# First two tiles of a spectral mixer normalized, turned and copied in three parts, x loaded tile by tile, last output in other pieces, and a new order of all work

## The chip, the cores and the metric

The kernel runs on one core of a Trainium2 chip. The metric is the device time of one execution in microseconds (us), as the median of a few runs. A core has five engines that work side by side and wait for each other through semaphores: TensorE (PE in the profile) multiplies matrices and turns tiles, VectorE (DVE) and ScalarE (ACT) do elementwise work, GpSimd (POOL) does a little, and SyncE (SP) issues the transfers (DMAs).

## The reference, cut to what matters

```python
xn = _layernorm(x, axis=-1)                     # x: 1 x 2048 x 640, bfloat16
return x + _A_ref(xn, A_w_r, A_w_i) + _B_ref(xn, B_w1, B_b1, B_w2, B_b2)

def _A_ref(x, w_r, w_i):                        # a filter in the 2-D spectrum
    X = rfft2(x.astype(float32)) * (w_r + 1j * w_i)
    return irfft2(X, s=(S, D)).astype(bfloat16)

def _B_ref(x, w1, b1, w2, b2):                  # a two-layer network
    h = gelu(x @ w1 + b1)                       # w1: 640 x 1536
    return h @ w2 + b2                          # w2: 1536 x 640
```

## The kernel before, in words

The 2048 rows of x are held as 16 tiles of 128 rows by 640 columns. Every tile is normalized, and its result goes two ways. For the network it is turned (columns to partitions, in five blocks of 128), because the matmuls with w1 need it so. For the spectrum it is folded twice by sums and differences, multiplied with tables of sines and cosines along the rows, then along the columns, filtered, and taken back.

Each piece of work is an operation with a name. Those that matter here, where `c` is a tile and `j` a block of 128 of its 640 columns:

- `x0`, `x1`, `x2`, `x4`, ... load x; from `x2` on two tiles in one transfer, so that `x14` brings tiles 14 and 15. `w1_00` to `w1_14` load w1 in two halves of five blocks.
- `st{c}` and `ag{c}` (DVE) take mean and variance. For tiles 0 and 1 `sq{c}` (ACT) and `rs{c}` (DVE) make the reciprocal root, for the others `ve` (DVE) and `rs` (POOL).
- `nm{c}` (DVE, L554) normalizes. In tile 0 it stands in two parts, columns 0 to 383 (`nm0`) and 384 to 639 (`nm0.3`).
- `tp{c}.{j}` (PE, L568) turns blocks of tiles 0 to 3 into a PSUM bank, one transpose each block, and `tc{c}.{j}` (DVE or ACT, L421/L422) copies them out. Tiles 4 to 15 are turned by DMA (`td{c}`, L560, issued on SP).
- `h{b}...` (PE) are the matmuls of the first layer. Blocks `h0` and `h1` are tiles 0 and 1 alone, taken row by row of w1, so that `h0.q.j` needs only block `j` of the turned tile and of w1. `h2` is tiles 2 and 3, `h3` is 4 and 5, `h4` is 6 and 7, `h5` is 8 to 11. `ge...` (ACT) is their gelu.
- `f1`, `f2` (DVE, L581 and L585) fold a pair of tiles, `G{c}` (PE) is the first spectral matmul of a tile and needs the folds of its pair. `f23` belongs to the tiles 6 and 7, and so to `G6` and `G7`.
- `k...`, `l...` (PE) are the second layer, `fin...` (PE) adds the last spectral matmul into the same bank, `os...` (DVE, L811) adds x and writes the result, `out...` (SP, L818) stores it.
- `idle0` and `idle1` are matmuls on a tile of zeros whose result nobody reads: 38 before the first data, and four between the turning of tile 0 and that of tile 1.

Nothing decides an order while the kernel runs. A table of some 900 entries, `ORDER`, names engine and operation one after the other, and `SLOTS` names the PSUM bank or buffer of each. Each engine takes its own entries strictly in this order; an operation that waits holds up all that stand behind it on its engine. A transfer too waits in SP's list until its data is ready.

Of the kernel before, what the change touches and what calls it, by code (L numbers as in the profile page):

```python
# [254 lines left out]
sp:w1_11 dve:ag1 dve:nm0 act:sq1 pe:b1mm dve:nm0.3 sp:w1_12 pe:tp0.0 dve:rs1 pe:tp0.3 dve:nm1 pe:idle1 sp:w1_13 act:tc0.3 dve:tc0.0 pe:tp1.0 act:b1cp
sp:w1_14 dve:f10.1 pe:h0.0.0 pe:h0.0.1 act:tc1.0 sp:x4 dve:f10.0 pe:h0.1.0 pe:h0.1.1 sp:x6 pe:h0.0.2 act:table1 pe:h0.1.2 pe:h1.1.0 sp:g pe:h1.1.1
pe:h1.1.2 pe:h1.0.0 sp:x8 pe:h1.0.1 dve:st3.1 pe:h1.0.2 sp:x10 dve:st3.0 pe:h1.0.3 pe:h0.0.3 sp:x12 dve:st2.1 pe:h1.1.3 pe:h0.0.4 pe:h1.0.4 dve:ag3
dve:st2.0 pe:h1.1.4 act:ge0.0 pe:h0.2.0 act:ge1.0 pe:h1.3.0 dve:ve3 dve:f20.11 pe:h0.3.0 act:ge1.4 pool:rs3 dve:ag2 dve:f20.10 pe:h0.2.1 act:ge1.5
pe:h0.1.3 dve:ve2 pe:h0.1.4 act:ge1.3 dve:f20.00 pe:h1.2.0 pool:rs2 act:ge0.1 pe:h1.3.1 dve:nm3 pe:h0.3.1 act:ge0.5 pe:h1.2.1 dve:f20.01 act:ge0.4
pe:h0.3.2 dve:nm2 act:ge0.2 pe:h0.2.2 pe:h0.2.3 pe:h0.2.4 dve:f11.0 pe:tp2.0 act:ge0.6 dve:f11.1 pe:h0.3.3 pe:h1.3.2 act:tc2.0 pe:tp3.0 dve:st4.0  # L260
pe:h1.2.2 dve:st4.1 pe:h1.2.3 act:tc3.0 pe:h0.3.4 pe:h1.3.3 dve:st5.0 pe:h1.2.4 act:ge1.2 pe:h1.3.4 dve:st5.1 pe:h2.4.0 act:ge1.7 act:ge1.8 pe:h2.4.3
dve:ag4 dve:ag5 act:ge1.1 pe:h2.8.0 dve:ve4 act:ge0.11 dve:f21.11 pe:h2.8.3 pool:rs4 dve:f21.00 act:ge1.6 pe:h2.9.0 dve:f21.10 act:ge0.3 pe:h2.9.3
act:ge0.7 pool:xbpad0b pe:h2.6.0 dve:nm4 act:ge1.10 pe:h2.6.3 dve:nm5 act:ge1.9 sp:td4 pe:h2.7.0 act:ge0.8 dve:f21.01 pe:h2.7.3 dve:st6.1 act:ge1.11
pe:h2.5.0 act:ge0.10 dve:st11.0 act:ge2.9 pe:G1 dve:f12.1 pe:h2.5.3 act:ge2.8 sp:td5 pe:h2.10.0 dve:st7.1 act:ge2.6 pe:h2.10.3 dve:st8.1 act:ge2.7
pe:h2.2.0 pe:G0 act:ge2.5 dve:f12.0 pe:h2.2.3 sp:x14 dve:st10.0 act:gx0.0 pe:h2.0.0 sp:w2_0 pe:h2.11.0 dve:st7.0 pe:h2.11.3 sp:W00m dve:st11.1
pe:h2.3.0 act:ge2.4 dve:st10.1 pe:h2.3.3 pe:h2.0.3 dve:f22.00 act:ge2.3 pe:h2.1.0 dve:st6.0 pe:h2.1.3 act:ge2.2 pe:h3.6.0 dve:f22.01 act:ge2.0 dve:ag6
dve:ag7 pe:h3.4.0 dve:f22.11 act:ge2.1 dve:ve6 dve:ag11 pe:G3 dve:f22.10 pool:rs6 pe:h3.6.3 dve:ag10 pe:G2 pe:h3.4.3 dve:nm6 act:gx1.0 pe:h3.5.0
dve:st9.0 pe:h3.7.0 sp:td6 dve:ve10 pe:h3.7.3 dve:st12.0 pool:rs10 pe:h3.8.0 dve:st8.0 act:ge2.10 pe:h3.8.3 pe:h3.9.0 act:ge2.11 dve:nm7 pe:h3.9.3
dve:nm10 sp:td7 pe:G4 act:ge3.9 dve:st9.1 pe:h3.5.3 pe:h3.0.0 dve:ag8 act:ge3.5 dve:ag9 pe:h3.0.3 dve:f13.0 pe:G5 act:ge3.4 dve:ve8 sp:td10 dve:st14.1
pe:h3.1.0 act:ge3.8 pool:rs8 pe:h3.1.3 dve:f13.1 act:gx2.0 pe:k1.0.0 dve:nm8 pe:k1.0.3 dve:f23.11 sp:td8 dve:nm11 pe:h3.2.0 act:ge3.1 dve:f23.01  # L270
dve:nm9 pe:h3.2.3 act:ge3.0 pe:h3.3.0 dve:f23.10 act:ge3.6 pe:h3.3.3 dve:f23.00 pe:h3.10.0 sp:td9 act:ge3.2 pe:h3.10.3 dve:f14.1 pe:h3.11.0 act:ge3.7
dve:f14.0 pe:h3.11.3 act:ge3.3 pe:G7 dve:f24.10 act:ge3.10 sp:td11 pe:G6 dve:st14.0 act:ge3.11 pe:h4.4.0 dve:st15.0 act:gx3.0 pe:h4.6.0 sp:w2_1
pe:h4.6.3 dve:f24.01 dve:f24.00 pe:h4.7.0 sp:W01p dve:f24.11 pe:h4.10.0 dve:ag14 dve:st15.1 pe:h4.7.3 pe:h4.10.3 dve:ag15 act:ge4.6 pe:h4.11.0
sp:bias2 dve:st13.1 pe:h4.11.3 act:ge4.7 sp:e dve:f15.1 pe:G9 act:ge4.10 pe:h4.4.3 dve:f15.0 sp:W11n pe:h4.5.0 act:ge0.9 dve:st12.1 act:ge4.11
pe:h4.5.3 sp:W10n pe:G8 dve:ag12 pe:h5.3.0 dve:st13.0 act:gx4.0 sp:W03n dve:ve14 dve:f25.00 pool:rs14 pe:h5.3.3 dve:f25.10 sp:W11p pe:h5.1.0 dve:ag13
act:ge5.3 dve:nm15 sp:W10m dve:ve12 pe:h5.1.3 dve:f25.01 pool:rs12 dve:f25.11 sp:W13p pe:h5.5.0 act:ge5.1 dve:nm13 sp:W01n pe:h5.5.3 act:ge4.5
dve:nm12 pe:h5.2.0 act:ge4.4 sp:W02p dve:f16.1 act:ge5.5 pe:G10 dve:nm14 sp:W00n pe:h5.2.3 dve:f16.0 sp:td15 pe:G11 dve:f26.01 act:ge5.2 pe:h4.2.0
dve:f26.11 dve:f26.00 pe:h4.2.3 dve:f26.10 pe:k1.0.6 dve:f17.0 sp:td13 pe:h5.4.0 dve:f17.1 pe:k1.0.9 dve:xs0 pe:h4.3.0 sp:td14 pe:h5.4.3 dve:kk1.0
# [573 lines left out]
```

## Time and profile before

| | us |
|---|---|
| median of 3 runs | 148.09 (147.81 to 149.21) |
| the profiled execution | 147.38 |
| its span | 146.1 |
| PE busy | 142.4 (97%) |
| DVE busy | 116.6 (80%) |
| ACT busy | 79.7 (55%) |

The span is what the profiler saw between the first and the last instruction; 1.28 us of the profiled execution lie around it. PE is busy nearly all the time, but its matmuls overlap in time, so this share alone does not say how closely they follow each other. The chain of waits says that, and so does the distance of the starts of equal matmuls.

### The profile page before, as it was taken

Reading aid. Unit: us, or ns where it says so; the run is one execution under the profiler, and the core shown is the slowest. Engines: PE = TensorE matmul, PEld = TensorE weight load, DVE = VectorE, ACT = ScalarE, POOL = GpSimd, SP = SyncE. Lnnn points to the kernel's source line nnn. Section 1 sums busy time; section 2 is a strip of 40 time slices with the busy share of each in tenths; the row PEclk is TensorE's granted clock in tenths of the full one; section 3 lists DMA queues with packets and bytes.
Section 4 is the critical chain, followed back from the end, with each engine's and each line's share of the span. In section 5 each row is a group of like instructions: output and inputs, shape, how many; then the busy total and the mean of one; then the engine's idle time right before and its main releaser. Section 6 shows DMA issues by size and latency. Waiting matters only on the chain.

```text
span 146.1 us, 4167 instructions
## 1 busy us (share of the span) xinstructions
PE 142.4 (97%) x1760; PEld 99.9 (68%) x1760; DVE 116.6 (80%) x272; ACT 79.7 (55%) x149; POOL 7.3 (5%) x24
## 2 busy tenths in 40 slices
PE   7999999999999999999999999999999999999993
PEld 7899889896659776546464443456678677767782
DVE  2999898999899486679899978840279979496993
ACT  3389997998747651578674787881043734100000
POOL 2031103102100000000000000000000000000000
PEclk9999999999999999999999999999999999999999
DMA  4999588698999999000000568267500022021334
GB/s 129 312 384 404 141 194 257 124 74 228 282 234 174 173 178 259 11 4 0 4 2 4 114 120 129 50 131 79 109 0 0 4 85 97 4 77 57 135 134 140
DMA packets 29226, 18.40 MB, mean 126 GB/s; under 512 B 20248, under 2 KB 27928, under 8 KB 29080
## 3 DMA queue, kind: packets, MB, share of 16 engines
q1 hardware_dynamic: 29184, 18.14, 52.5%
q8 instruction: 14, 0.23, 0.7%
q14 instruction: 4, 0.03, 0.1%
q10 hardware_dynamic: 24, 0.00, 0.0%
HBM read 10.92 MB, written 2.62 MB: 93 GB/s over the span
## 4 chain that ended last, share of the span: by engine, by line
PE 95%; DVE 2%; DMA 2%; issue 0%
PE ps L411 93%; DMA X<-in_A_x_dram 2%; DVE U L522 1%; PE ps L568 1%; DVE W L811 0%; DVE T L554 0%; DVE mv L524 0%; DVE rstd L528 0%
## 5 line engine op out<-in xcount | busy, mean ns | idle before, releaser
L411 PE MATMUL ps<-W,gT 128*128 128x256 bf16 (+3 forms) x396 | 58.8, 296 | 0.0
L411 PE MATMUL ps<-xnT,W 128*128 128x256 bf16 (+2 forms) x420 | 57.8, 288 | 0.0
L411 PEld LDWEIGHTS ps<-W,gT 128*128 128x128 bf16 x396 | 36.8, 98 | 15.3 <-issue 1.2
L411 PEld LDWEIGHTS ps<-xnT,W 128*128 128x128 bf16 x420 | 34.4, 98 | 15.2 <-issue 2.4
L640 ACT ACTIVATE gT<-ps,b1col 128x256 bf16<-128x256 f32 (+2 forms) x84 | 36.7, 522 | 8.5 <-PE ps L411 8.4
L421 ACT ACTIVATE Wf<-ps 128x960 bf16<-128x960 f32 (+1 forms) x9 | 7.6, 880 | 17.2 <-PE ps L411 17.2
L522 DVE BATCH_NORM_STATS2 U<-X 128x6 f32<-128x320 bf16 x32 | 14.1, 475 | 2.6 <-DMA X<-in_A_x_dram 2.6
L421 ACT ACTIVATE T<-ps 128x644 bf16<-128x644 f32 (+2 forms) x17 | 9.3, 581 | 8.0 <-PE ps L411 8.0
L421 ACT ACTIVATE XV<-ps 128x1280 bf16<-128x1280 f32 (+1 forms) x8 | 9.5, 1193 | 1.3 <-PE ps L411 1.3
L585 DVE TENSOR_TENSOR T<-T 128x128 bf16<-128x128 bf16 (+1 forms) x32 | 9.0, 311 | 0.1
L811 DVE TENSOR_TENSOR W<-ps,xnT 128x256 bf16<-128x256 f32 (+1 forms) x16 | 7.4, 481 | 1.4 <-DMA out_dram<-W 1.2
L554 DVE TENSOR_SCALAR T<-X,mv,rstd 128x640 bf16<-128x640 bf16 (+2 forms) x17 | 7.0, 433 | 1.6 <-POOL rstd L533 1.3
L422 DVE CAST T<-ps 128x644 bf16<-128x644 f32 x7 | 5.8, 828 | 2.9 <-PE ps L411 2.8
L801 DVE TENSOR_TENSOR xnT<-ps,X 128x384 f32<-128x384 f32 (+1 forms) x16 | 7.7, 484 | 0.6 <-PE ps L411 0.3
L421 ACT ACTIVATE Xb<-ps 128x960 bf16<-128x960 f32 x5 | 6.2, 1262 | 3.4 <-PE ps L411 3.4
L411 PE MATMUL ps<-Wf,htab 128*128 128x256 bf16 (+3 forms) x33 | 8.0, 296 | 0.0
L533 POOL TENSOR_TENSOR rstd<-ve,mhalf 128x2 f32<-128x2 f32 (+1 forms) x8 | 6.1, 768 | 29.1 <-DVE ve L532 29.1
L700 DVE TENSOR_TENSOR T<-T 128x644 bf16<-128x644 bf16 x16 | 7.4, 485 | 0.1
L581 DVE TENSOR_TENSOR T<-T 128x640 bf16<-128x640 bf16 x16 | 7.3, 480 | 0.1
L411 PE MATMUL ps<-EB,XV 32*128 32x160 bf16 (+1 forms) x128 | 7.2, 232 | 0.0
L411 PEld LDWEIGHTS ps<-EB,XV 32*128 32x128 bf16 (+1 forms) x128 | 5.5, 95 | 2.2 <-ACT Xb L421 0.5
L774 DVE TENSOR_TENSOR Wf<-Wf 128x960 bf16<-128x960 bf16 (+1 forms) x12 | 6.8, 595 | 0.1
(62 smaller groups left out, 127.0 us busy)
## 6 DMA issues: line engine op xcount, KB each, us to landing
out_dram<-W SPq DMA_DIRECT2D x15, 160.0 KB, 1.8
X<-in_A_x_dram SPq DMA_DIRECT2D x7, 320.0 KB, 6.6
W<-in_B_w_dram SPq DMA_DIRECT2D x10, 192.0 KB, 4.3
W<-in_B_w_dram SPq DMA_DIRECT2D x2, 960.0 KB, 6.2
Wf<-in_A_w_r_dram SPq DMA_DIRECT2D x7, 160.5 KB, 5.9
Wf<-in_A_w_i_dram SPq DMA_DIRECT2D x7, 160.5 KB, 4.3
gtab<-c_G SPq DMA_DIRECT2D x1, 512.0 KB, 7.4
htab<-c_H SPq DMA_DIRECT2D x1, 512.0 KB, 5.4
```

The source lines that it names most:

```text
L411: ins = e.matmul(o_, lhsT=lw, rhs=rh, start=st, stop=sp_, skip_group_check=True)
L421: return e.activation(dst(), src(), ACT.Copy)
L522: K.op(f"st{c}.{h}", "dve", lambda e, _, c=c, h=h: e.bn_stats(stats[:, c, 6 * h:6 * h + 6], view(X, c * D + H2 * h, [[1, H2]])), reads=[B_ ...
L533: K.op(f"rs{c0}", "pool", lambda e, _, a=a, b=b: e.tensor_tensor(out=rstd[:, a:b], in0=ve[:, a:b], in1=mhalf[:, a:b], op=ALU.pow), reads=[ ...
L554: norm = K.op(f"nm{c}" if not a else f"nm{c}.3", "dve", lambda e, _, c=c, n=n, a=a, b=b, xnv=xnv: e.tensor_scalar(out=xnv(n, a, [[1, b - a ...
L581: K.op(f"f1{pair}.{k}", "dve", lambda e, _, k=k, op=op, xnv=xnv, x1v=x1v: e.tensor_tensor(out=x1v(H2 * k, [[D, 2], [1, H2]]), in0=xnv(0, 0 ...
L585: ring_ops.append(K.op(f"f2{pair}.{k}{i}", "dve", lambda e, _, op=op, x1v=x1v, xfv=xfv, o_=o_, o0=o0, o1=o1, w=w: e.tensor_tensor(out=xfv( ...
L640: K.op(f"ge{bi}.{fc}", "act", lambda e, _, c0=c0, nt=nt, fc=fc, f0=f0, hps=hps: e.activation(gT[:, fc, 128 * c0:128 * (c0 + nt)], psb(hps. ...
L700: return e.tensor_tensor(out=rows, in0=rows, in1=view(TT, TB.slot * 4 * KP + r * KP, [[2 * KP, 2], [1, KP]]), op=op)
L774: K.op(f"yf{gi}.{k}", "dve", lambda e, _, k=k, op=op, y2=y2, yf=yf, n=n: e.tensor_tensor(out=view(Wf, YF + yf.slot * 3 * D + (D - 1) * k, ...
L801: K.op(f"kk{c}.{o0}", "dve", lambda e, _, kps=kps, c=c, home=home, o0=o0, w=w: e.tensor_tensor(out=home[:, o0 // 128:(o0 + w) // 128], in0 ...
L811: K.op(f"os{c}.{o0}", "dve", lambda e, _, c=c, os_=os_, fps=fps, o0=o0, w=w, kept=kept, home=home if kept else None: e.tensor_tensor(out=( ...
```

## The change

Tiles 0 and 1 are now both treated in three parts, of one, two and two blocks of 128 columns: three normalizations, three turns (in three banks), three copies each. The matmuls of `h0` and `h1` wait for the part that holds their block. `idle1` is gone. Tiles 2 and 3 are loaded by two transfers, `x2` and `x3`, of which the second stands behind the first half of w1. The last output tile, 15, is finished in pieces of 384, 160 and 96 columns instead of 320, 160 and 160. One more group of output tiles gets a copy (`xr1`) of the block of 128 rows that its matmuls use in quarters. The whole table of the order is new, and 29 copies changed between DVE and ACT.

```diff
+PARTS = (0, 1, 3, 5)
-NEAR = (2, 3, 4, 5)
+NEAR = (1, 2, 3, 4, 5)
-PIECES = {15: [(0, H2), (H2, Q4), (H2 + Q4, Q4)]}
-WARM = (38, 4)
+PIECES = {15: [(0, 384), (384, 160), (544, 96)]}
+WARM = 38
 ORDER = """
-act:table0 pool:id1 sp:w1_00 sp:w1_01 sp:w1_02 sp:x2 dve:st0.0 dve:st0.1 sp:w1_03 dve:st1.1 sp:w1_04 dve:ag0 dve:st1.0 sp:w1_10 act:sq0 dve:rs0
...
-        for j in range(5):
-            if j == 3:
-                first(load_x(2, 2))
-            first(load_w1(0, j))
-        for j in range(5):
-            first(load_w1(1, j))
+        for h in range(2):
+            for j in range(5):
+                if (h, j) in ((0, 3), (1, 0)):
+                    first(load_x(2 + h, 1))
+                first(load_w1(h, j))
...
-        B_xnT = [[K.buf(f"xnT{c}.0"), K.buf(f"xnT{c}.3")] for c in range(16)]
+        B_xnT = [[K.buf(f"xnT{c}.{a}") for a in PARTS[:-1]] for c in range(16)]
...
-                parts = ((0, 384), (384, D)) if c == 0 else ((0, D),)
+                parts = [(128 * a, 128 * b) for a, b in zip(PARTS, PARTS[1:])] if c < 2 else [(0, D)]
...
-                for j0, j1, engs in ((0, 3, "dve"), (3, 5, "act")) if c == 0 else ((0, 5, "dve act"),):
+                for k, (j0, j1) in enumerate((a // 128, b // 128) for a, b in parts):
...
-                    if j0:
-                        idle("idle1", WARM[1], gate=[tp])
-                    K.op(f"tc{c}.{j0}", engs, copy(
+                    K.op(f"tc{c}.{j0}", "dve act", copy(
...
-                                reads=[B_w1s[h][j], B_xnT[c0][j // 3]], writes=[banks[q]], gate=l1_of[bi][-2:][:1] if j else []))
+                                reads=[B_w1s[h][j], B_xnT[c0][(j + 1) // 2]], writes=[banks[q]], gate=l1_of[bi][-2:][:1] if j else []))
```

Two places show what the new order does. The first is the start of PE's list, with what each instruction waits for (`EB` holds the zeros and the unit matrix, `T` the normalized tile, `xnT` the turned one, `W` is w1). Before:

```order
L411 MATMUL ps<-EB 128x128 x37
L411 MATMUL ps<-EB 128x12 [waits d_bias1,s_pool]
L568 MATMUL ps<-EB,T 128x128 [waits s_dve]
L568 MATMUL ps<-EB,T 128x128 x2
L568 MATMUL ps<-EB,T 128x128 [waits s_dve]
L568 MATMUL ps<-EB,T 128x128
L411 MATMUL ps<-EB 128x128 x4
L568 MATMUL ps<-EB,T 128x128 [waits s_dve]
L568 MATMUL ps<-EB,T 128x128 x4
L411 MATMUL ps<-xnT,W 128x128 [waits d_w1_00,s_dve]
```

The same place after:

```order
L413 MATMUL ps<-EB 128x12 [waits d_bias1,s_pool]
L569 MATMUL ps<-EB,T 128x128 [waits s_dve] x2
L569 MATMUL ps<-EB,T 128x128
L569 MATMUL ps<-EB,T 128x128 [waits s_dve]
L569 MATMUL ps<-EB,T 128x128
L413 MATMUL ps<-xnT,W 128x128 [waits d_w1_00,s_act,s_dve]
L413 MATMUL ps<-xnT,W 128x128 x2
L569 MATMUL ps<-EB,T 128x128 [waits s_dve]
L413 MATMUL ps<-xnT,W 128x128 x3
L569 MATMUL ps<-EB,T 128x128 [waits s_act,s_dve]
```

The four matmuls on zeros are gone, and the first six matmuls of the first layer stand before and between the turns of tile 1.

The second place is DVE's list between the statistics of tiles 8 to 13 and the normalization of tile 6 (`d_x10`, `d_x12`, `d_x14` are the landings of these loads of x; L522 and L523 are `st`, L581 and L580 `f1`, L585 and L584 `f2`, L554 and L555 `nm`). Before, from `nm6` to `st14.1`:

```order
L554 TENSOR_SCALAR T<-X,mv,rstd 128x640 [waits s_pool]
L522 BN_STATS U<-X 128x6
L532 TENSOR_SCALAR ve<-mv 128x2 [waits s_dve]
L522 BN_STATS U<-X 128x6 [waits d_x12]
L522 BN_STATS U<-X 128x6
L554 TENSOR_SCALAR T<-X,mv,rstd 128x640
L554 TENSOR_SCALAR T<-X,mv,rstd 128x640 [waits d_td4,d_td5,s_pool]
L522 BN_STATS U<-X 128x6
L524 BN_AGGR mv<-U 128x2 [waits s_dve] x2
L581 TENSOR_TENSOR T<-T 128x2x320
L532 TENSOR_SCALAR ve<-mv 128x2 [waits s_dve]
L522 BN_STATS U<-X 128x6 [waits d_x14]
```

After, from `f12.0` to `nm6`:

```order
L580 TENSOR_TENSOR T<-T 128x2x320 [waits s_dve]
L523 BN_STATS U<-X 128x6 x3
L523 BN_STATS U<-X 128x6 [waits d_x14]
L523 BN_STATS U<-X 128x6
L525 BN_AGGR mv<-U 128x2 [waits s_dve]
L580 TENSOR_TENSOR T<-T 128x2x320
L525 BN_AGGR mv<-U 128x2
L533 TENSOR_SCALAR ve<-mv 128x2 [waits s_dve]
L584 TENSOR_TENSOR T<-T 128x2x2x128 [waits s_pe]
L584 TENSOR_TENSOR T<-T 128x2x2x32
L584 TENSOR_TENSOR T<-T 128x2x2x128
L555 TENSOR_SCALAR T<-X,mv,rstd 128x640 [waits s_pool]
```

The first use of `x14` stood behind the normalizations of the tiles 6, 7 and 10 and the first sums of the pair of tiles 6 and 7; it is now `st15.0`, ahead of all of them, and everything behind it on DVE waits for that load. In SP's list `x14` stands right behind `td5` in both kernels.

More of the change, by code (lines that the diff above doesn't have):

```diff
@@ L255 @@
[L255 to L278, printed above, removed]
@@ L314 @@
+pe:fin15.544 sp:out14.0 dve:os15.544 sp:out15.544
 """
 SLOTS = """
-idle0:0 b1ps:1 xn0:0 x10:0 xf0:0 tps0.0:2 tps0.3:3 idle1:0 tps1.0:4 aps0:0 xn1:1 x11:0 xf1:1 tps2.0:7 tps3.0:5 aps1:0 xn2:2 x12:0 xf2:0 aps2:0 xn3:3
-x13:0 xf3:1 aps3:0 xn4:0 x14:0 xf4:0 aps4:0 xn5:2 x15:0 xf5:1 aps5:0 xn6:0 x16:0 xf6:0 aps6:0 xn7:1 x17:0 xf7:1 aps7:0 hps0_0:5 hps0_1:6 hps0_2:0
-hps0_3:3 hps1_0:4 hps1_1:7 hps1_2:2 hps1_3:1 hps2_0:4 hps2_2:5 hps2_4:7 hps2_6:4 hps2_8:5 hps2_10:6 hps3_0:6 hps3_2:4 hps3_4:5 hps3_6:7 hps3_8:4
@@ L327 @@
-kps10_384:6 fps10_0:1 fps10_384:4 yo4:0 y24:0 yf4:0 eps4:0 xr4:1 os11:3 kps11_0:7 kps11_384:7 fps11_0:6 fps11_384:1 os12:2 fps12_0:0 fps12_384:3
-os13:0 fps13_0:4 fps13_384:5 yo5:0 y25:0 yf5:0 eps5:0 xr5:0 os14:0 fps14_0:7 fps14_384:6 os15:2 fps15_0:0 fps15_320:1 fps15_480:4
+idle0:0 b1ps:1 xn0:0 x10:0 xf0:0 tps0.0:2 tps0.1:3 tps0.3:0 tps1.0:2 tps1.1:3 tps1.3:5 aps0:0 xn1:1 x11:0 xf1:1 tps2.0:7 tps3.0:4 aps1:0 xn2:2 x12:0
+xf2:0 aps2:0 xn3:3 x13:0 xf3:1 aps3:0 xn4:1 x14:0 xf4:0 aps4:0 xn5:0 x15:0 xf5:1 aps5:0 xn6:2 x16:0 xf6:0 aps6:0 xn7:3 x17:0 xf7:1 aps7:0 hps0_0:1
@@ L446, in idle @@
             pe(name, lambda: [(psb(b.slot, [[1, 128]]), warm, warm, True, True) for _ in range(n)], reads=[B_warm], writes=[b], **kw)
-        idle("idle0", WARM[0])
+        idle("idle0", WARM)
         B_b1, B_b2b = K.buf("b1t"), K.buf("b2")
```

124 lines of the change are left out of this document (76 added, 48 removed).

## The prediction

> **What bounds the kernel now.** I read the chain of waits first, in order of time, since it says what set the end.
>
> ```profile
> 0.73 2.31 DMA X<-in_A_x_dram
> 3.07 1.28 DVE U L522 x3
> ...
> 5.09 0.32 DVE T L554
> 5.46 0.72 PE ps L568 x5
> ...
> 6.94 5.36 PE ps L411 x96
> ...
> 13.20 46.73 PE ps L411 x485
> 59.93 83.62 PE ps L411 x1059
> 143.57 0.32 DVE W L811
> ```
>
> From 5.46 us on the chain never leaves PE until the last sum at 143.57 us. So a change can win in three places alone: ahead of the first useful matmul, in the count and width of PE's matmuls, and behind the last one. Everywhere else it can only lose, by making PE wait. The timeline of the first microseconds comes next; PE's rows of the same time are merged over equal forms.
>
> ```profile
> 5.46 0.72 PE L568 MATMUL ps<-EB,T 128*128 128x128 bf16 x5
> 5.76 0.45 DVE L554 TENSOR_SCALAR T<-X,mv,rstd 128x640 bf16<-128x640 bf16 x1
> 5.97 0.63 PE L411 MATMUL ps<-EB 128*128 128x128 bf16 x4
> 6.13 0.35 DVE L422 COPY xnT<-ps 128x384 bf16<-128x384 bf16 x1
> 6.39 0.55 PE L568 MATMUL ps<-EB,T 128*128 128x128 bf16 x5
> 6.78 5.52 PE L411 MATMUL ps<-xnT,W 128*128 128x128 bf16 x96
> ```
>
> Two things are to be seen. The four `idle1` matmuls stand between the turns of tiles 0 and 1, for 6.39 - 5.97 = 0.42 us. And PE changes its pace there: the starts of the four lie (0.63 - 0.31) / 3 = 0.107 us apart, taking 0.31 us for one of them from the row of `idle0` (`EB`) below, and those of the first layer (5.52 - 0.22) / 95 = 0.056, with 0.22 us for one. The change falls between 6.4 and 6.7 us. All of them have the same 128 x 128 form.
>
> ```profile
> L411 PE MATMUL ps<-EB 128*128 128x128 bf16 x23 | 2.9, 314 | 0.0
> L411 PE MATMUL ps<-xnT,W 128*128 128x128 bf16 x94 | 5.4, 219 | 0.0
> ```
>
> The end is read from the timeline too. SP issues five stores in a row there:
>
> ```profile
> 142.44 2.45 SPq L818 DMA_DIRECT2D out_dram<-W  x5
> 142.47 0.99 PE L411 MATMUL ps<-W,gT 128*128 128x160 bf16 x12
> 143.30 0.23 PE L411 MATMUL ps<-Wf,htab 128*128 128x160 bf16 x1
> out_dram<-W SPq DMA_DIRECT2D x2, 40.0 KB, 1.6
> ```
>
> Five issues in 2.45 us put the last one at about 144.4, half a microsecond behind the end of the last sum (143.57 + 0.32 = 143.89). It lands 1.6 us later, and the span ends at 146.1. From the start of the last matmul to the end of the span it takes 146.1 - 143.30 = 2.8 us.
>
> **The start.** Up to `nm0` DVE does the same as before. The normalizations by size:
>
> ```profile
> L554 DVE TENSOR_SCALAR T<-X,mv,rstd 128x640 bf16<-128x640 bf16 x1 | 0.4, 445 | 0.0
> L554 DVE TENSOR_SCALAR T<-X,mv,rstd 128x384 bf16<-128x384 bf16 x1 | 0.4, 378 | 0.0
> L554 DVE TENSOR_SCALAR T<-X,mv,rstd 128x256 bf16<-128x256 bf16 x1 | 0.3, 339 | 0.0
> 5.02 0.64 DVE L554 TENSOR_SCALAR T<-X,mv,rstd 128x384 bf16<-128x384 bf16 x2
> ```
>
> 256 columns more cost 67 ns (445 - 378), so a part of 128 takes about 0.31 us, and as the pair in the last row overlaps by 0.08 us, its successor starts after 0.23. A part of 256 hands on after 0.26. Walked from 5.02: the three parts of tile 0 end at 5.33, 5.59 and 5.85. In the rows `nm1` starts 0.1 us behind the end of the pair (5.76 against 5.66), with `rs1` between; here I put `tc0.0` there, at about 5.85, to end near 6.1 (0.35 us for three times the columns before), and tile 1's parts from 6.0 on, to end at 6.31, 6.57 and 6.83. PE follows a part after 0.05 us (5.46 against 5.41). One block is turned at 5.38, two at 5.65, two at 5.9; the first three matmuls of the layer run from 6.13 to 6.45, a turn to 6.56, three matmuls to about 6.75, and the last turns wait for 6.83 and end near 7.0. Six matmuls of the layer are then done, worth 6 x 0.056 = 0.34, which puts the layer's start at 6.66 in the old reckoning, against 6.78: **-0.12 us**. Of the 0.42 us of `idle1` the rest is not won, because tile 1's normalization, not PE, is then late. Bounds: -0.42, and +0.1 in an execution where PE's pace is already 0.056 at 5.4 (the last turns then wait for 6.83 just the same).
>
> DVE pays for it. Six parts cost 2 x (0.23 + 0.26 + 0.26) = 1.5 us of it where three cost 0.30 + 0.26 + 0.36 = 0.92, and a copy of tile 1 is added: it is about **0.65 us later** from here on. The loads of w1 have cover: `x2` is half as large ahead of the fourth block of w1, and `x3` only fills the place of the other half further on.
>
> **DVE and the load x14.** This is where that delay can reach PE. The new order puts `st15.0` ahead of the normalizations of tiles 6 to 11.
>
> ```profile
> 18.10 0.58 SPq L406 DMA_DIRECT2D X<-in_A_x_dram  x1
> X<-in_A_x_dram SPq DMA_DIRECT2D x1, 320.0 KB, 3.8
> 19.00:20.00 1.00, 1.00 (x12) 1.00 0.90 93
> 20.00:21.00 1.00, 1.00 (x11) 1.00 0.62 114
> 21.00:22.00 1.00, 1.00 (x13) 1.00 1.04 393
> q8 instruction: 1, 0.02, 2.9%
> ```
>
> `x14` lands at 18.10 + 3.8 = 21.9; the last column of the three windows (GB/s) shows that it hardly moves for two microseconds, behind `td5` and one packet of 0.02 MB on an instruction queue, and then goes at 393. The Trainium skill (Runtime: NRT & Kernel Launch, Instruction fetch mechanics) says that an engine's program is fetched in 16 KiB blocks at a cost that is mostly hidden. By that rule alone the load would not be late and this whole term zero; the trace has the slow windows at that packet, without showing which of the two made them.
>
> These rows give the pieces of DVE's work from there on, and the place of `G6` and `G7` on PE:
>
> ```profile
> 18.75 1.66 DVE L522 BATCH_NORM_STATS2 U<-X 128x6 f32<-128x320 bf16 x4
> 29.07 0.89 DVE L581 TENSOR_TENSOR T<-T 128x640 bf16<-128x640 bf16 x2
> 28.29 0.75 DVE L585 TENSOR_TENSOR T<-T 128x512 bf16<-128x512 bf16 x2
> 27.30 0.21 DVE L585 TENSOR_TENSOR T<-T 128x128 bf16<-128x128 bf16 x1
> 24.27 0.79 DVE L554 TENSOR_SCALAR T<-X,mv,rstd 128x640 bf16<-128x640 bf16 x2
> 13.38 0.33 DVE L524 BATCH_NORM_AGGREGATE mv<-U 128x2 f32<-128x12 f32 x2
> 21.50 0.17 DVE L532 TENSOR_SCALAR ve<-mv 128x2 f32<-128x2 f32 x1
> 22.65 0.45 DVE L554 TENSOR_SCALAR T<-X,mv,rstd 128x640 bf16<-128x640 bf16 x1 [0.47 <-POOL rstd L533]
> 29.80 0.72 PE L411 MATMUL ps<-gtab,T 128*128 128x128 bf16 x10
> ```
>
> Before, the first user of `x14` comes four microseconds after it landed. At 18.75 (first row) DVE had four `st` of the tiles from 6 on and two `f1` behind it; ahead of `st15.0` stand ten and one. That is 18.75 + 6 x 0.40 - 0.40 = 20.75, or 21.4 with the 0.65: DVE comes before the load and stands.
>
> Behind that start come, up to the end of the sum that `G6` needs (`f23.00`): five `st`, three `f1`, seven `f2`, four `nm`, six `ag`, three `ve`, and one more `f2`. From start to start they take 0.40, 0.40, 0.33 (0.13 for a small `f2`, 0.21 less the overlap), 0.36, 0.13 and 0.07 us: 2.0 + 1.2 + 1.0 + 0.5 + 1.4 + 0.8 + 0.2 + 0.42 = 7.5. `nm6` starts 1.15 us behind its `ve6` (22.65 against 21.50, through POOL); only 0.8 us of `f2` lie between them, so 0.35 is added: 7.9. PE comes to these two `G` (29.80, x10) about 0.12 earlier than before, at 29.7. They wait if `x14` lands after 29.7 - 7.9 = 21.8. It is issued behind `td5`, which comes up to 0.65 later, so at 18.1 to 18.75. Nearest row: 3.8 us, so 21.9 to 22.55, a wait of 0.1 to 0.75; if nothing stands in its way, the 2.3 us of the first load of x (160 KB) and 0.4 for its second half at 393 GB/s make 20.8 to 21.45, and the wait is nothing. I take 22.2, so 0.4, and 0.1 for `G4` and `G9`, which follow on the same engine: **+0.5 us**, bounds 0 and +1.0. The first `h5`, which needs the last of `td8` to `td11`, is pushed by the same wait and so covered.
>
> **Width of the last tile.** The columns are the same, but 12 matmuls of 96 columns may not run at 96/160 of the 0.069 us that the rows of 160 give ((0.99 - 0.23) / 11); between 0.041 and the 0.056 of 128 columns the loss is 0 to 12 x 0.015 = 0.18. I take **+0.08**. `xr1` adds a copy ahead of matmuls of the same number: nothing on PE, hidden by the second layer's matmuls between; the copies that changed engine likewise.
>
> **The tail.** The last sum falls from 160 to 96 columns, under 0.1 us. But the end hangs on SP: again five stores stand one behind the other, with the store of tile 14 right ahead of the last. The five begin when the second half of tile 10 is summed; counted from there the last issue comes 0.3 to 0.4 us behind the last sum where it was 0.5: **-0.2 us**, bounds -0.6 (no queue at all) and +0.1.
>
> **Sum:** -0.12 + 0.5 + 0.08 - 0.2 = +0.26 us on the profiled execution's 147.38 us, 147.64. That execution lies 0.71 under the median of the runs shown (148.09), so I add the sum to the median: **148.35, say 148.4 us**, no change that can be told. About 1% (1.5 us) is what a measurement of this kernel can tell from none.
>
> **Rivals.**
>
> *The load is not late* (chance 0.27). Issued later, `x14` meets less of the slow stretch, which ended at 21; from there 320 KB take 0.8 us at 393 GB/s. It lands by 21.8, and `G6` waits for nothing. Against it: `td5` shifts too. Then 148.35 - 0.5 = 147.85, and 147.15 if start and tail reach their lower bounds as well (0.3 and 0.4 more). Below 146.6 it hardly comes.
>
> *The load is fully late* (0.2). `x14` lands at 22.6 or after, as the packet and `td5` shift with it. DVE stands up to 1.8 us, `G6` waits 0.8 and `G9` and the transposes behind it some more: +1.0, and at most the whole stand. For it: the 3.8 us of the only row. The point from which it decides is a landing at 22.5; time 148.9 to 149.6, slower than before.
>
> *PE's pace changes later* (0.07).
>
> ```profile
> 1.02 4.35 PE L411 MATMUL ps<-EB 128*128 128x128 bf16 x39 [1.02 <-DVE EB L427]
> ```
>
> PE is at work from 1.02 and turned at about 6.6, 5.6 us later. Without `idle1` it stands some 0.2 us more between the parts. If that made the 5.6 us run anew from the first turn at 5.4, the pace would change at 11.0, and 4.4 us would go at half speed: +2.2, so 150.5, slower. Against it: before, PE stood too, from 5.37 (1.02 + 4.35) to 5.46, and the pace changed all the same. The Trainium skill (TensorE: Matmul & The Clock Gate, What's actually happening) has a mechanism: a free-running window of about 3.4 us that must be busy. By that rule the turn would come one window later if the busy share fell short, an estimated +1.7 us. The granted-clock column reads 1.00 all along and cannot show it; the distance of the starts does.
>
> *The change does not do what it says* (0.06). DVE paces the start and SP the tail, so both terms are nothing: 148.7.
>
> **How the numbers follow.** The forecast itself has 0.4 and a range of its own of 148.0 to 148.8. The range for 8 in 10 takes most of both load rivals: 147.4 to 149.4; the pace rival and the far ends are left out. Slower by over 1% (above 149.6) is the pace rival and the far end of the full delay: 0.11. Faster by over 1%: 0.04. The rest, 0.85, within 1%.
>
> **What would show it.** In the changed kernel: the first `xnT,W` matmul near 6.1 and the layer gapless from 7.0; a DVE wait of 1 to 1.7 us for a load of x near 21 us, and PE idle ahead of a `gtab,T` group near 30 us by about 0.4; from the last matmul's start to the end 2.6 us. I am wrong if that DVE wait is missing, if starts stay 0.107 apart beyond 7 us, or if PE waits at a place not named here.

## The result and the profile after

The changed kernel takes 154.88 us (median; 153.09 to 156.19) beside 148.0 us of the kernel before on the same chip: the ratio is 1.042, with a 95% interval of 1.038 to 1.046. It is slower by 4%, where the prediction had no change (148.4 us, range 147.4 to 149.4). The profiled execution took 155.04 us, its span is 153.4 us, 7.3 us longer than that of before (146.1).

The chain of waits of the changed kernel, its last part in order of time, no longer runs on PE from the start to the end:

```profile
34.83 0.58 SPq L408
35.45 11.04 DMA W<-in_B_w_dram
46.54 100.35 PE ps L413 x1244
146.89 3.20 DMA out_dram<-W
150.11 0.56 DVE W L810
```

A load of w2 that takes 11.04 us ends a wait of PE at 46.54, and a store of 3.20 us stands ahead of the last sums. Neither is in the prediction. PE's first microseconds, from the timeline:

```profile
5.36 0.80 PE L569 MATMUL ps<-EB,T 128*128 128x128 bf16 x5
6.06 0.34 PE L413 MATMUL ps<-xnT,W 128*128 128x128 bf16 x3
...
6.54 0.54 PE L569 MATMUL ps<-EB,T 128*128 128x128 bf16 x4
6.92 1.28 PE L413 MATMUL ps<-xnT,W 128*128 128x128 bf16 x20
```

The layer runs on from 6.92 with six matmuls done, worth 6 x 0.056 us, so it starts at 6.58 in the old reckoning, where before it was 6.78: the start won 0.20 us. Its pace from 6.92 on is the full one: (1.28 - 0.22) / 19 = 0.056 us. It was full already at 6.06, where three matmuls take 0.34 us, (0.34 - 0.22) / 2 = 0.06 us from start to start; before, the pace had changed between 6.4 and 6.7 us only.

The timeline around `x14`, with the rows of SP, DVE and PE:

```profile
16.19 3.61 SPq L561 DMA_TRANSPOSE xnT<-T  x2
19.84 0.58 SPq L408 DMA_DIRECT2D X<-in_A_x_dram  x1
19.66 1.27 DVE L523 BATCH_NORM_STATS2 U<-X 128x6 f32<-128x320 bf16 x3
23.18 0.89 DVE L523 BATCH_NORM_STATS2 U<-X 128x6 f32<-128x320 bf16 x2 [2.25 <-DMA X<-in_A_x_dram]
23.75 2.35 PE L413 MATMUL ps<-xnT,W 128*128 128x256 bf16 x20
26.80 0.45 PE L413 MATMUL ps<-gtab,T 128*128 128x128 bf16 x5 [0.71 <-DVE T L584]
29.77 0.93 PE L413 MATMUL ps<-xnT,W 128*128 128x256 bf16 x7
31.13 0.73 PE L413 MATMUL ps<-gtab,T 128*128 128x128 bf16 x10 [0.44 <-DVE T L584]
```

DVE stands 2.25 us for `x14`. A matmul of 256 columns starts 0.109 us behind the one ahead of it ((2.35 - 0.27) / 19, with 0.27 us for one), so PE could have gone on at 23.75 + 20 x 0.109 = 25.93 and at 29.77 + 7 x 0.109 = 30.53; it lost 0.87 us ahead of `G4` and 0.60 us ahead of `G6`.

The stand for w2, first as PE's timeline, then as windows of one microsecond (behind the window: busy shares and counts of PE, PE's weight loads, DVE, ACT and POOL, the granted clock, the share of the DMA engines, GB/s):

```profile
42.68 0.72 PE L413 MATMUL ps<-gtab,T 128*128 128x128 bf16 x10
46.54 3.06 PE L413 MATMUL ps<-W,gT 128*128 128x384 bf16 x9 [3.14 <-DMA W<-in_B_w_dram]
49.39 1.29 PE L413 MATMUL ps<-xnT,W 128*128 128x512 bf16 x6
```

```profile
46.00:47.00 1.00, 0.46 (x2) 0.28 (x3) 1.00 (x2) 0.00 (x0) 0.00 (x0) 0.74 1.07 177
47.00:48.00 1.00, 1.00 (x5) 0.45 (x3) 0.52 (x2) 0.00 (x0) 0.00 (x0) 0.50 2.19 142
48.00:49.00 1.00, 1.00 (x4) 0.45 (x3) 0.00 (x0) 0.00 (x0) 0.00 (x0) 0.50 1.16 133
49.00:50.00 1.00, 1.00 (x4) 0.44 (x3) 0.00 (x0) 0.00 (x0) 0.00 (x0) 0.56 0.90 116
```

PE could have gone on at 42.68 + 10 x 0.056 = 43.24: it stood 3.30 us for `k1.0.6`. Then the granted clock is 0.50 until about 49.9, so half of some 3.3 us is lost, 1.6. Nine matmuls of 384 columns take 49.39 - 46.54 = 2.85 us there; in a run below the same nine take 1.47.

The end, from the timeline:

```profile
149.35 0.67 PE L413 MATMUL ps<-W,gT 128*128 128x96 bf16 x12
149.86 0.21 PE L413 MATMUL ps<-Wf,htab 128*128 128x96 bf16 x1
150.11 1.29 DVE L810 TENSOR_TENSOR W<-ps,X 128x384 bf16<-128x384 f32 x4 [1.16 <-DMA out_dram<-W]
```

From the last matmul's start to the end it takes 153.4 - 149.86 = 3.54 us, 0.74 more than before (2.8): DVE stands 1.16 us for a store, and four sums are left when PE is done. Together: -0.20 + 0.87 + 0.60 + 3.30 + 1.6 + 0.74 = 6.9 of the 7.3 us of this execution. The half pace is not in every run of the changed kernel: the mean granted clock over the run is 0.978 to 0.986 in three of the six and 0.996 or 0.997 in the others.

### The profile page after: what moved, and what is told of

Same layout as the page of the kernel before. It is cut to its first block, busy times and chain, and to the rows that moved or that the text cites. A ratio compares the mean times of both kernels' runs of the same rounds, so it can differ in the third digit from the quotient of the medians.

```text
span 153.4 us, 4180 instructions
## 1 busy us (share of the span) xinstructions
PE 144.8 (94%) x1756; PEld 99.1 (65%) x1756; DVE 121.0 (79%) x278; ACT 79.4 (52%) x150; POOL 7.4 (5%) x24
## 3 DMA queue, kind: packets, MB, share of 16 engines
HBM read 10.92 MB, written 2.62 MB: 88 GB/s over the span
## 4 chain that ended last, share of the span: by engine, by line
PE 65%; DVE 16%; DMA 13%; SPq 2%; POOL 1%; issue 1%; DVEq 0%
PE ps L413 65%; DMA W<-in_B_w_dram 7%; DVE U L523 5%; DMA X<-in_A_x_dram 4%; DVE T L555 3%; DVE T L580 2%; DMA out_dram<-W 2%; SPq L561 2%; DVE T L584 2%; POOL rstd L534 1%; DVE mv L525 1%; DVE W L810 1%; DVE ve L533 1%; SPq L408 0%; DVE xnT L424 0%
## 5 line engine op out<-in xcount | busy, mean ns | idle before, releaser
L413 PE MATMUL ps<-W,gT 128*128 128x384 bf16 (+3 forms) x396 | 61.0, 300 | 3.1 <-DMA W<-in_B_w_dram 3.1
L413 PEld LDWEIGHTS ps<-xnT,W 128*128 128x128 bf16 x420 | 34.9, 98 | 15.9 <-issue 2.3
L523 DVE BATCH_NORM_STATS2 U<-X 128x6 f32<-128x320 bf16 x32 | 14.1, 480 | 4.3 <-DMA X<-in_A_x_dram 4.3
L423 ACT ACTIVATE Wf<-ps 128x960 bf16<-128x960 f32 (+1 forms) x8 | 6.7, 869 | 10.9 <-PE ps L413 5.8
L423 ACT ACTIVATE XV<-ps 128x1280 bf16<-128x1280 f32 (+1 forms) x7 | 8.1, 1154 | 2.6 <-PE ps L413 2.6
L584 DVE TENSOR_TENSOR T<-T 128x128 bf16<-128x128 bf16 (+1 forms) x32 | 8.9, 315 | 0.0
L424 DVE CAST T<-ps 128x644 bf16<-128x644 f32 (+2 forms) x8 | 5.9, 742 | 3.7 <-PE ps L413 3.6
L555 DVE TENSOR_SCALAR T<-X,mv,rstd 128x640 bf16<-128x640 bf16 (+2 forms) x20 | 7.8, 408 | 0.3 <-POOL rstd L534 0.2
L424 DVE CAST U<-ps 128x512 bf16<-128x512 f32 (+2 forms) x11 | 5.2, 522 | 3.3 <-PE ps L413 3.3
L413 PE MATMUL ps<-Wf,htab 128*128 128x384 bf16 (+3 forms) x33 | 7.8, 295 | 0.0
L423 ACT ACTIVATE Xb<-ps 128x960 bf16<-128x960 f32 x4 | 5.0, 1258 | 5.3 <-PE ps L413 5.3
L580 DVE TENSOR_TENSOR T<-T 128x640 bf16<-128x640 bf16 x16 | 7.5, 477 | 0.1
L413 PE MATMUL ps<-gtab,T 128*128 128x128 bf16 x80 | 6.5, 219 | 1.1 <-DVE T L584 1.1
```

What stands on the lines that cost most here:

```text
L413: ins = e.matmul(o_, lhsT=lw, rhs=rh, start=st, stop=sp_, skip_group_check=True)
L423: return e.activation(dst(), src(), ACT.Copy)
L424: return e.tensor_copy(dst(), src())
L523: K.op(f"st{c}.{h}", "dve", lambda e, _, c=c, h=h: e.bn_stats(stats[:, c, 6 * h:6 * h + 6], view(X, c * D + H2 * h, [[1, H2]])), reads=[B_ ...
L555: norm = K.op(f"nm{c}.{a // 128}" if a else f"nm{c}", "dve", lambda e, _, c=c, n=n, a=a, b=b, xnv=xnv: e.tensor_scalar(out=xnv(n, a, [[1, ...
L580: K.op(f"f1{pair}.{k}", "dve", lambda e, _, k=k, op=op, xnv=xnv, x1v=x1v: e.tensor_tensor(out=x1v(H2 * k, [[D, 2], [1, H2]]), in0=xnv(0, 0 ...
```

## The experiments

Every kernel is the changed one with the edit shown, except where the kernel before is named. The diffs of the order show the entries of one engine alone, with those of the others between them left out. The ratios are to the kernel before on the same chip, with 95% intervals; the changed kernel's own is 1.042. A hundredth of it is 1.5 us.

**The load x14.** `x14` issued ahead of `td4` and `td5` in place of behind them:

```diff
-sp:td4 sp:td5 sp:x14 sp:w2_0
+sp:x14 sp:td4 sp:td5 sp:w2_0
```

> The changed kernel, with the load x14 issued ahead of td4 instead of behind td5; nothing else moves. Theory A (the late load): x14 lands before 20 us, DVE no longer stands 2.2 us ahead of st15.0, so G4 and G6 wait for nothing (1.6 us less), td6 to td9 and with them w2_1 go out about 2 us earlier (33.3 instead of 35.5), w2_1 lands by about 40 and k1.0.6 waits for nothing, so that PE's pace does not fall either: about 148.2 us. Rival B (the load of w2_1 is slow in itself, because of what stands behind it in SP's list): w2_1 still takes 11 us, lands near 44.3, PE stands 2 to 3 us and may lose pace: 151 to 153 us.

152.28 us, 1.020 (1.011 to 1.028). The 2.25 us of DVE and both waits ahead of `G4` and `G6` are gone; PE still stands 2.25 us for w2, and the time is far above 148.2. So the wait for `x14` isn't all. The other way to the same end is to leave the load and take its first use later:

```diff
-dve:st15.0
...
 dve:nm9
+dve:st15.0
```

> The changed kernel, with st15.0 on DVE behind nm9 instead of ahead of st9.1; x14 is issued where it was. Theory A: same gain as with the earlier load, as only DVE's stand counts: G4 and G6 wait less than 0.2 us, w2_1 goes out near 33.3, total about 148.2 us. Rival B: the waits of G4 and G6 go (1.6 us), w2_1 stays 11 us under way: 151 to 153 us. A third reading, that x14 itself disturbs the transposes, would leave this kernel slow and the one with the early load fast.

151.51 us, 1.016 (1.006 to 1.027). Its timeline on PE:

```profile
41.12 0.72 PE L413 MATMUL ps<-gtab,T 128*128 128x128 bf16 x10
43.94 1.64 PE L413 MATMUL ps<-W,gT 128*128 128x384 bf16 x9 [2.10 <-DMA W<-in_B_w_dram]
45.41 0.81 PE L413 MATMUL ps<-xnT,W 128*128 128x512 bf16 x4
```

Behind a stand of 43.94 - 41.68 = 2.26 us the nine matmuls take 1.47 us, the full pace. So the place of `st15.0` costs 1.5 us ahead of the two `G`, 1.0 of the stand for w2, and the half pace: 4.1 of the loss by these terms, 0.026 or 3.8 us by the ratios. The rest has another cause. The place of `st15.0` alone, in the kernel before:

```diff
 dve:st10.1
+dve:st15.0
...
-dve:st15.0
```

> The kernel before, with one entry moved: st15.0 on DVE right behind st10.1, ahead of the load's landing, as in the changed kernel. Theory A: DVE stands from 20.3 to 21.9, nm6 to nm11, the transposes and w2_1 shift by 1.5 us; f23.00 ends at 30.6 and G7 waits 0.8 us, w2_1 goes out at 34.2, lands at 40.2 against a k1.0.6 at 40.4: +0.8 us, about 148.9. Rival B, with a w2_1 that takes 11 us when it is issued late: PE stands 4 us more and loses pace, 153 or more. If the place of st15.0 does not matter: 148.0.

151.07 us, 1.012 (1.004 to 1.020), span 150.1. DVE stands and hands it on to PE ahead of `G6` and `G7`, as in the changed kernel:

```profile
23.61 0.50 DVE L522 BATCH_NORM_STATS2 U<-X 128x6 f32<-128x320 bf16 x1 [1.96 <-DMA X<-in_A_x_dram]
```

```profile
32.78 0.73 PE L411 MATMUL ps<-gtab,T 128*128 128x128 bf16 x10 [1.46 <-DVE T L585]
```

That is between the two expectations: 1.8 us by the ratio, and 1.46 us in the row of PE. The profiled execution has two more stands of PE, 0.79 us for w1 at 9.97 and 0.51 us for the transposes of tiles 4 and 5 at 22.52. Both end before DVE's stand does (23.61), so the moved entry did not make them. `w2_1` lands 5.7 us after its issue there, and PE does not wait for it. The wait for `x14` alone doesn't make that load late.

**The load w2_1.** Issued right behind `w2_0`, where it was behind `td9` and `bias2`:

```diff
-sp:x14 sp:w2_0 sp:W00m
+sp:x14 sp:w2_0 sp:w2_1 sp:W00m
...
-sp:td9 sp:bias2 sp:w2_1 sp:W11p
+sp:td9 sp:bias2 sp:W11p
```

> The changed kernel, with the load w2_1 issued right behind w2_0, ahead of td6 to td9, instead of behind them. Theory A and rival B alike: w2_1 lands before 33 us, the stand of 3.3 us ahead of k1.0.6 and the 1.7 us of halved pace behind it go, the waits of G4 and G6 stay (1.6 us): about 150 us. It tells how much of the loss passes through SP's list. If the transposes now wait behind 960 KB, h4 or h5 would stand instead, up to 2 us.

150.21 us, 1.008 (1.003 to 1.013). That is what was expected. No stand for w2 is left; the waits ahead of the two `G` and the late end are still there. Why did the load take 11 us where it took 6.0 before? Two things stand differently around it: `bias2` is ahead of it, where it came behind, and it is issued 2.8 us later. Two kernels tell these apart. In one, `w2_1` and `bias2` change places:

```diff
-sp:td9 sp:bias2 sp:w2_1 sp:W11p
+sp:td9 sp:w2_1 sp:bias2 sp:W11p
```

> The changed kernel with one edit: SP issues w2_1 ahead of bias2 instead of right behind it, as the kernel before has it. Theory A, that the load of bias2 (128 copies of one row) right ahead of w2_1 makes its transfer slow: w2_1 is issued near 34.8, lands 6 us later as before, near 41, ahead of k1.0.6 (43.2); the stand of 3.3 us and the half pace behind it (1.7 us) go, 154.9 - 5.0 = 149.9 us. Theory B, that the loads issued behind w2_1 take the queue's time: it still lands 11 us after its issue, near 45.9, PE stands some 2.7 us, 152.5 to 154 us.

150.8 us, 1.018 (1.012 to 1.024); `w2_1` lands 5.7 us after its issue, and nothing waits for it, as theory A has it. The median lies 0.9 us above its time. The profiled execution (151.68 us) has a wait of 1.35 us for the transposes of tiles 4 and 5 that the changed kernel's profile does not have: DVE stood 1.06 us for a load of x at 13.77, and `td4` went out at 17.41 instead of 16.19. Whether the other three runs have it is not shown. In the other, a load of 200 KB with a row of its own for each partition takes the place of `bias2`, which is one row of 1,280 bytes read 128 times:

```diff
-sp:td9 sp:bias2 sp:w2_1 sp:W11p sp:W01n sp:e
+sp:td9 sp:e sp:w2_1 sp:bias2 sp:W11p sp:W01n
```

> The changed kernel with two loads moved: the load of e (200 KB, a row of its own for each partition) is issued right ahead of w2_1, and bias2 (one row for all 128 partitions) right behind it. Theory A, that it is the copying of one row that slows what is queued behind it: w2_1 lands about 6 us after its issue, near 41.5, before k1.0.6 asks for it, and the time is near that of w2_swap, 150.8 us. Theory B, that any load of such a size right ahead of w2_1 slows it: it lands 10 to 11 us after its issue, PE stands 3 us ahead of k1.0.6, 154 to 155 us.

150.85 us, 1.016 (1.009 to 1.023). The issues of these loads (kilobytes, us to landing), of this kernel, then of the changed one, and last that of `w2_1` in the kernel before:

```profile
W<-in_B_w_dram SPq DMA_DIRECT2D x1, 960.0 KB, 5.5
EB<-c_E SPq DMA_DIRECT2D x1, 200.0 KB, 2.8
U<-in_B_b_dram SPq DMA_DIRECT2D x1, 160.0 KB, 6.8
```

```profile
W<-in_B_w_dram SPq DMA_DIRECT2D x1, 960.0 KB, 11.0
...
U<-in_B_b_dram SPq DMA_DIRECT2D x1, 160.0 KB, 5.8
```

```profile
W<-in_B_w_dram SPq DMA_DIRECT2D x1, 960.0 KB, 6.0
```

With the larger load ahead of it `w2_1` takes 5.5 us, with `bias2` ahead of it 11.0. So it is that load, not any load, and not the moment of the issue. The windows show where the time goes. Of the changed kernel, whose `bias2` and `w2_1` are issued at 34.83 and 35.45, and of the kernel before, which issues `w2_1` at 32.63:

```profile
36.00:37.00 1.00, 1.00 (x11) 0.67 (x9) 0.93 (x4) 0.48 (x2) 0.50 (x1) 1.00 0.11 44
37.00:38.00 1.00, 1.00 (x7) 0.46 (x5) 1.00 (x1) 0.09 (x1) 0.36 (x1) 1.00 0.32 91
38.00:39.00 1.00, 1.00 (x6) 0.42 (x5) 1.00 (x3) 0.61 (x2) 0.00 (x0) 1.00 0.60 169
39.00:40.00 1.00, 1.00 (x6) 0.49 (x5) 1.00 (x6) 0.68 (x1) 0.76 (x1) 1.00 0.78 259
```

```profile
34.00:35.00 1.00, 1.00 (x10) 0.59 (x9) 0.96 (x6) 0.77 (x2) 0.17 (x1) 1.00 0.65 127
35.00:36.00 1.00, 1.00 (x7) 0.47 (x5) 0.87 (x4) 1.00 (x2) 0.63 (x1) 1.00 1.05 388
```

Behind `bias2` the queue moves 44, 91, 169 and 259 GB/s in these four microseconds. About three microseconds after the issue of `w2_1` it is at 169 (38 to 39), where before it was at 388 (35 to 36). By 39 us five loads that were issued later share it. How much of the 11 us is the slow start and how much this sharing was not tried apart.

**The half pace.** 24 matmuls whose result nobody reads, ahead of `k1.0.6`:

```diff
+        hb = K.buf("hold1", psum, 1, ANY)
+        pe("hold1", lambda: [(psb(hb.slot, [[1, 128]]), gT[:, 0, 0:128], W2[:, 0, 0:128], True, True) for _ in range(24)],
+           reads=[B_w2[0], B_gT[0, 0]], writes=[hb])
...
-pe:G10 pe:k1.0.6
+pe:G10 pe:hold1 pe:k1.0.6
```

> The changed kernel with 24 matmuls of 128 columns whose result nobody reads (1.3 us of PE), placed ahead of k1.0.6, so that PE stands some 2 us there in one piece instead of 3.3. Theory A, that the long stand makes PE go on at half pace: no run shows it, the mean granted clock is 0.995 or more in each (it was 0.985, 0.978 and 0.986 in three of six runs of the changed kernel), and the median falls by some 1 to 1.7 us to 153.2 to 153.9. Theory B, that the half pace has another cause (the loads that move at that time, or any stand): clocks of 0.98 to 0.99 in about half the runs, and 154.9 us.

152.93 us, 1.029 (1.024 to 1.035), and the mean granted clock is 1.0 in all six runs.

```profile
42.69 1.50 PE L413 MATMUL ps<-W,gT 128*128 128x128 bf16 x24
45.68 1.64 PE L413 MATMUL ps<-W,gT 128*128 128x384 bf16 x9 [1.49 <-DMA W<-in_B_w_dram]
47.37 0.82 PE L413 MATMUL ps<-xnT,W 128*128 128x512 bf16 x5
```

PE has 24 matmuls more to do, and the kernel is faster than the changed one: 0.012 by the ratios, 1.8 us. The stand is 45.68 - (42.69 + 24 x 0.056) = 1.65 us, and behind it the nine matmuls of 384 columns take at most 47.37 - 45.68 = 1.69 us. With the stand broken the half pace came in no run. The 1.8 us are not all its price, since only three of the six runs of the changed kernel had the low clock. In the profile of `hold` the end is shorter too, without the wait for a store:

```profile
146.40 1.49 DVE L813 TENSOR_TENSOR W<-ps,X 128x384 bf16<-128x384 f32 x4
```

The length of a stand does not decide alone. In the profiles the half pace did not come at 1.65 and 2.26 us, though one of the four runs of `x14_early`, whose profile has a stand of 2.4 us, has a mean clock of 0.989. In `tail5`, the next kernel, the profiled execution stood 3.2 us without it, while the other three runs have mean clocks of 0.987 to 0.989. And behind PE's last matmul of the changed kernel (149.86) the clock is at 0.50 again from 152.29, after some 2.2 us without work.

The times at which the clock changes, read from short windows, suggest why. From 46.48 to 49.89 are 3.41 us, and from 49.89 to 152.29 are 102.4, which is 30 times 3.413. So the changes lie on a raster of 3.41 us, and the stand from 43.24 to 46.54 fills nearly all of one step of it (43.07 to 46.48). In the profile of `tail5` the clock changes at 150.12; 31 steps earlier is 44.3, in the middle of its stand from 42.8 to 45.9, and neither step is empty. That is an estimate from two profiles; no run moved a stand against the raster.

**The end.** A fifth output buffer, so that tile 14 need not wait until tile 8 is stored:

```diff
-("os", 4)
+("os", 5)
...
-view(W1, os_.slot * D + o0, [[1, w]])
+view(W1, (os_.slot + 4 * (os_.slot > 3)) * D + o0, [[1, w]])
...
-os14:3
+os14:4
```

> The changed kernel with one edit: the sums of tile 14 get a fifth output buffer, so that they do not wait for the store of tile 8. Theory A, that this wait sets the end: from the last matmul's start to the end 2.6 us instead of 3.56, 154.9 - 0.9 = 154.0 us. Theory B, that the issues on SP set it: the same time, 154.9 us.

154.08 us, 1.035 (1.027 to 1.043). The chain no longer passes through a store:

```profile
139.97 7.88 PE ps L413 x75
...
147.88 0.26 DVE W L810
```

From the last matmul's start (147.63) to the end of the span (150.5) it takes 2.87 us, where the changed kernel's profile has 3.54 and theory A had 2.6. The median is the 154.0 us that theory A gave, though the intervals of the two kernels overlap; the pair below, with and without this buffer, shows the difference more clearly. The wait needs a slow store as well as the shared buffer: in `hold`, with four buffers, the store of tile 8 lands 1.8 us after its issue instead of 3.2, and DVE does not wait for it.

**The edits together.** `st15.0` behind `nm9`, and `w2_1` ahead of `bias2`; the diffs are those above.

> The changed kernel with st15.0 moved behind nm9 and w2_1 ahead of bias2. If bias2 is what makes w2_1 slow: 151.5 (st15_late) less its stand of 2.3 us, 149.2 us. If it is the loads behind w2_1: the same as st15_late or up to 0.6 less, 150.9 to 151.5.

148.45 us, 1.003 (0.999 to 1.006). With the fifth buffer as well:

> The changed kernel with all three edits: st15.0 behind nm9, w2_1 ahead of bias2, a fifth output buffer. If these three name the whole loss, what is left is the start (0.12 to 0.15 us shorter than before) and a tail 0.2 shorter: 148.2 us, 0.3 below the kernel before. If something else is still in it: 149 us or more.

147.83 us, 0.998 (0.995 to 1.001), span 146.3. The fifth buffer is worth 148.45 - 147.83 = 0.6 us. Three edits undo the whole loss, with the start, the loads and the widths of the change kept. The kernel is not to be told from the one before (0.7 us less to 0.1 more), so a gain of the 0.2 us that the start won may be left or not. Its end:

```profile
143.75 0.21 PE L413 MATMUL ps<-Wf,htab 128*128 128x96 bf16 x1
```

146.3 - 143.75 = 2.55 us from the last matmul's start, where before it was 2.8.

**The start alone.** The kernel before with its start as in the changed kernel (the six parts, `x2` and `x3` apart, no `idle1`), the rest of its order kept:

```diff
-dve:nm0 dve:nm0.3 dve:rs1 dve:nm1 dve:tc0.0 dve:f10.1 dve:f10.0 dve:st3.1
+dve:nm0 dve:nm0.1 dve:nm0.3 dve:rs1 dve:tc0.0 dve:nm1 dve:nm1.1 dve:nm1.3 dve:f10.0 dve:f10.1 dve:tc1.3 dve:st3.1
...
-pe:tp0.0 pe:tp0.3 pe:idle1 pe:tp1.0 pe:h0.0.0 pe:h0.0.1
+pe:tp0.0 pe:tp0.1 pe:tp0.3 pe:h0.0.0 pe:tp1.0 pe:h0.1.0 pe:tp1.1 pe:tp1.3 pe:h0.1.1 pe:h0.0.1
```

> The kernel before with the start alone changed: tiles 0 and 1 normalized, turned and copied in three parts each, tiles 2 and 3 loaded one by one, no idle matmuls between the turns; all that follows in the order of before. Theory A, that the start is worth 0.12 to 0.15 us and the 0.6 us that DVE pays for it costs nothing while st15.0 stays where it was: 147.85 us where before has 148.0. Theory B, that DVE's delay reaches PE by itself (later transposes, a later issue of w2_1): 148.3 to 149 us.

149.79 us, 1.008 (1.005 to 1.011): slower by 0.8%. Two rows of its timeline, DVE and PE:

```profile
8.66 1.28 DVE L523 BATCH_NORM_STATS2 U<-X 128x6 f32<-128x320 bf16 x3 [0.84 <-DMA X<-in_A_x_dram]
23.00 0.81 PE L413 MATMUL ps<-xnT,W 128*128 128x256 bf16 x6 [1.32 <-DMA xnT<-T]
```

DVE stands 0.84 us for tile 3, which the old order takes ahead of tile 2 but which now arrives behind it; later PE stands for the transposes of tiles 4 and 5. So the tiles are taken in the order in which they arrive:

```diff
-dve:st3.1 dve:st3.0 dve:st2.1 dve:ag3 dve:st2.0
+dve:st2.1 dve:st2.0 dve:st3.1 dve:ag2 dve:st3.0
...
```

> As start_only, but tile 2, which now arrives ahead of tile 3, is also taken first on DVE, so that DVE does not stand for tile 3 (0.84 us in start_only). DVE is then some 0.7 us behind the kernel before where it was 1.5 us. Theory A, that the start itself is worth its 0.12 to 0.15 us and start_only lost by that stand alone: td4 and td5 are issued near 16.1 and 17.4, PE does not stand ahead of the second layer's matmuls of tiles 4 and 5 near 21.5, 147.8 to 148.2 us. Theory B, that 0.7 us on DVE is enough to bring td5 behind the packet of instructions near 18.5 and to make PE stand 0.5 us or more there: 148.5 to 149.5 us.

148.57 us, 1.000 (0.997 to 1.003). This lies between what the two theories gave and settles neither: the profiled execution has a stand of PE at the place that theory B named, and the median is that of the kernel before. The row names ACT, but the later of the two transposes lands at 22.34, right before PE goes on.

```profile
16.45 3.70 SPq L561 DMA_TRANSPOSE xnT<-T  x2
22.43 0.82 PE L413 MATMUL ps<-xnT,W 128*128 128x256 bf16 x6 [1.23 <-ACT gT L639]
```

The two transposes hold SP for 3.70 us, where they took 2.62 in the kernel before, with a packet of 16 KB on the instruction queue near them in both. The fourteen profiles fall in two groups. In eight the packet moves 0.5 to 2.2 us after the issue of the first of the two transposes, and the pair holds SP for 3.1 to 3.8 us; in six, the kernel before among them, it moves after 2.3 us or later, and the pair takes 2.6. That the packet is the cause was not tried.

## Why the prediction was wrong, point by point

**The start** was right in its sum: -0.12 expected, -0.20 us in the profile, the first matmul of the layer at 6.06 (6.13 expected), gapless from 6.92 (7.0). One step of it was not: the working lets the first three matmuls run at the slow pace until 6.45, but the pace was full from 6.06 on, earlier than in the profile before. So part of the 0.20 may be the luck of two executions. What DVE pays for it was right too: `td4` is issued at 16.19 instead of 15.44, 0.75 us later where 0.65 was expected. Whether the gain outlives that delay is not shown: the median of `start_st2` is that of the kernel before, with an interval of 0.4 us to either side.

**DVE and the load x14**: the mechanism was right and its size wrong in this execution. The place, the stand of DVE and the two waits of PE are those forecast. The prediction took a landing at 22.2 and half a microsecond. Its upper bound for the issue was 18.75; it was 19.84, since `td4` and `td5` took 3.61 us on SP and not 2.62. The stand was 2.25 us where 1 to 1.7 was the forecast, and PE lost 1.5 where 0.5 was taken. Its rival "the load is fully late", with a landing at 22.6 or after, is what happened, and its price of 1.0 was 0.5 short. The work behind the load was sized well: from its landing (23.16) to `G6` (31.13) it takes 7.97 us, where 7.9 was worked out. In `e_ahead`, `tail5` and `hold`, which have the same order up to there, the same two transposes take 2.6 us on SP; `x14` lands at 22.3 to 22.6, DVE stands 1.4 to 1.7 us, and PE loses 0.5 to 0.9, close to the forecast. So the missing microsecond is that of the transposes, which comes in some executions and not in others.

**The step that failed** is the sentence that the first `h5` is "pushed by the same wait and so covered", and with it the sum's silence on what stands further down in SP's list. The wait that DVE passes on delays the transposes `td6` to `td11`, and everything queued behind them on SP. There stands `w2_1`, issued at 35.45 instead of 32.63, and now behind `bias2`; the prediction put this new order of SP's loads at nothing. I followed `x14` through SP's list and stopped there. PE's stand of 3.30 us and the half pace of 1.6, two thirds of the loss in the profile, come from this. Of the two causes of the late landing, the later issue is worth 2.8 us and the neighbour 5.0 (11.0 against 6.0 to land); without the neighbour nothing waits, in `w2_swap` and `e_ahead` alike, though the issue is as late there (35.66 and 34.94).

**PE's pace** was a rival at the wrong place: it had the pace turn later at the start, where it turned earlier, and it fell in the middle instead. The Trainium skill (TensorE: Matmul & The Clock Gate, What's actually happening) says that the array falls back to half its clock after an idle window of about 3.4 us and needs a busy one to recover. The trace agrees with the size: the clock was at 0.50 for 3.41 us, from 46.48 to 49.89. The stand before it was shorter, 3.30 us, and the end of the kernel (2.2 us) and `tail5` (3.2 us without a fall) show that its length alone does not decide.

**Width of the last tile**: twelve matmuls of 96 columns take (0.67 - 0.21) / 11 = 0.042 us each, which is 96/160 of 0.069. The term is 0, its lower bound, not +0.08.

**The tail** had the wrong sign: -0.2 expected, +0.74 us found. "The end hangs on SP" left out that the sums need a free output buffer. The new table of buffers gives tile 14 the one of tile 8, whose store takes 3.2 us and lands 1.16 us after DVE could have taken that sum. With a buffer of its own the end is 2.55 us in `all3`, the 2.6 that the prediction had.

**The condition for being wrong**, "PE waits at a place not named here", is the one that came true.

## What to carry to other kernels

A wait on one engine is not priced by its first victim alone: follow each queue behind it to its end, its loads above all, and compare what now stands next to each of them. A new table of buffers is a part of the change like the order: for each buffer, look for the last store that must be done before its next use. And a stand of some three microseconds on PE can cost more than its length, so breaking it with work that nobody needs may pay.
